# Adding the pixel to a depthwise convolution in PSUM by a second matmul, in a windowed-attention kernel

## The chip, the cores and the metric

The kernel runs on one core of a Trainium2 chip. The metric is device time in microseconds of one execution. All times below are medians of executions in the undisturbed ("fast") state unless said otherwise. Engines are named as the profile names them: PE is TensorE's matmul, PEld its weight load, DVE is VectorE, ACT is ScalarE, POOL is GpSimd, SP is SyncE. A matmul has a stationary operand (its weights, loaded first) and a moving operand (the columns streamed past them); its sums land in PSUM, and copying them out of there is called an evacuation. The granted clock is the share of TensorE's full clock that the profile shows.

## The reference

An image of 511 x 511 pixels with 192 channels goes through a 3 x 3 depthwise convolution that is added to it, a layer norm, attention with 4 heads inside windows of 7 x 7 pixels, an output projection, and a residual addition:

```
x0 = x + depthwise3x3(x, dw_pe)          # this case is about this line
h  = layernorm(x0)
qkv = windows(h) @ w_qkv                 # 73 x 73 windows of 49 tokens
out = softmax(q @ k.T * scale) @ v @ w_o
return x0 + unwindow(out)
```

All inputs are bf16.

## The kernel before

The 5329 windows are handled in 42 blocks of 128. While a block goes through attention in groups of 8 windows, the next block's convolution and statistics are slipped in between. Two copies of x are loaded for a block:

- `XP`, by plane: 81 partitions (the 9 x 9 pixels that a window's convolution touches), then 128 windows, then 192 channels. It feeds the convolution.
- `XC`, by token: 128 partitions (windows), then 49 tokens, then 192 channels. The convolution is added to it, giving x0.

The convolution of one channel is one matmul: the stationary operand is `XP[0:81, :, c]`, 128 weights that lie 192 elements (384 bytes) apart, and the moving operand is a tap matrix of 81 x 49. Twenty channels share a PSUM tile (there are four tiles for the whole kernel), and VectorE adds the tile to `XC`:

```python
def load_xc(blk):
    ...   # 16 windows at a time, on the GpSimd queue
    nc.gpsimd.dma_start(out=xc[...], in_=xw[a, b0 + o : b0 + o + nb])

def conv_tile(blk, it):
    ...
    ps = PS.next()
    for cc in range(ncn):
        nc.tensor.matmul(ps[:, col : col + S], lhsT=XP[0:KP, :, c], rhs=T[0:KP, c, :], start=True, stop=True)
    nc.vector.tensor_tensor(out=xc[...], in0=<the PSUM tile>, in1=xc[...], op=ALU.add)
    ...
```

`XC` has two buffers, so the load for a block waits until the store of the block two before it has left the buffer, and VectorE's addition waits for the load.

## Time and profile before

| | before |
|---|---|
| time, median of 2 | 5348.66 us (5340.74 to 5356.59) |
| busy share PE / DVE / ACT / POOL | 84% / 72% / 51% / 14% |
| mean granted clock | 0.824 |
| convolution matmuls, each with its own load | 8064 |
| DMA moved | 375 MB |

The busy shares are averages over stages with different limits. One block of some 127 us has a convolution stage in which TensorE is busy nearly all the time (38.22 of 39 us in the block read below), and an attention stage in which TensorE, VectorE and ScalarE take turns. The prediction below shows the lines and how they are read.

### The profile page before, as it was taken

The page shows a single profiled execution, that of the slowest core. Times are in us where ns is not written, and L with a number is a line of the kernel's source. Part 1 is how long each engine was busy: PE and PEld are TensorE (multiplying, and loading weights), DVE is VectorE, ACT ScalarE, POOL GpSimd, SP SyncE. Part 2 cuts the span into 40 slices and gives each one's busy share as a digit, 9 for nine tenths or more (in the row PEclk, how much of TensorE's full clock was granted, in tenths as well). Part 3 has the DMA queues.
Part 4 walks back from the last instruction along what each step waited for, and adds up shares of the span by engine and source line. Part 5 has one row for each costly group of instructions (what it writes and reads, how often), then busy time and mean ns, then how long its engine had stood idle before and what let it go on. Part 6 is the DMA issues. An engine that isn't in the chain of part 4 may idle for free.

```text
span 5337.2 us, 148265 instructions
## 1 busy us (share of the span) xinstructions
PE 4490.1 (84%) x65427; PEld 3661.5 (69%) x65427; DVE 3816.7 (72%) x6912; ACT 2744.5 (51%) x3385; POOL 758.0 (14%) x833
## 2 busy tenths in 40 slices
PE   2788888888888888888988888888888888888887
PEld 1666676667776676677776777767666776677776
DVE  6776777767776777777677777777777777767776
ACT  1554555545555555555555455555555555545555
POOL 1111111111111111111111111111111111111120
PEclk9887888887778887888788877788888888877888
DMA  6554445554455555554455544455555445544431
GB/s 67 51 75 70 68 71 80 82 73 68 68 68 70 71 72 74 71 74 71 68 73 91 75 68 68 68 72 72 74 72 72 73 70 78 85 74 67 68 48 32
DMA packets 512613, 375.27 MB, mean 70 GB/s; under 512 B 453129, under 2 KB 453321, under 8 KB 511958
## 3 DMA queue, kind: packets, MB, share of 16 engines
q1 hardware_dynamic: 480918, 265.08, 38.1%
q0 software_dynamic: 30592, 100.32, 10.6%
q8 instruction: 514, 8.42, 0.7%
q14 instruction: 141, 1.16, 0.1%
q10 hardware_dynamic: 448, 0.30, 0.0%
HBM read 265.31 MB, written 100.27 MB: 68 GB/s over the span
## 4 chain that ended last, share of the span: by engine, by line
PE 44%; DVE 16%; ACT 14%; DMA 12%; SPq 9%; issue 4%; POOL 1%; DVEq 0%; ACTq 0%; POOLq 0%
PE ps L412 12%; PE ps L282 8%; SPq L396 7%; DMA out_dram<-XC 7%; PE ps L369 6%; DMA XC<-in_x_dram 5%; PE ps L453 5%; PE ps L532 4%; DVE kT L424 4%; ACT hT L355 4%; DVE Qb L422 3%; PE ps L431 2%; DVE XC L284 2%; PE ps L560 2%; ACT kT L426 2%
## 5 line engine op out<-in xcount | busy, mean ns | idle before, releaser
L412 PE MATMUL ps<-hT,Wqk 96*128 96x392 bf16 x5336 | 1233.5, 380 | 76.7 <-DVE XC L284 62.2
L478 ACT ACTIVATE PT<-ps 128x784 bf16<-128x784 f32 x667 | 552.7, 829 | 1095.3 <-PE ps L453 1080.3
L421 ACT CAST Qb<-ps 64x784 bf16<-64x784 f32 x667 | 555.3, 833 | 657.5 <-PE ps L412 655.7
L412 PEld LDWEIGHTS <-Wqk 96*128 96x128 bf16 x5336 | 529.4, 108 | 486.1 <-issue 252.5
L284 DVE TENSOR_TENSOR XC<-ps,XC 128x980 bf16<-128x980 f32 x378 | 437.9, 1176 | 503.0 <-PE ps L282 247.2
L282 PE MATMUL ps<-T,XP 81*128 81x49 bf16 x8064 | 744.0, 264 | 55.5 <-DMA XP<-in_x_dram 55.5
L567 ACT CAST OT<-ps 96x784 bf16<-96x784 f32 x667 | 541.0, 811 | 456.0 <-PE ps L560 452.4
L282 PEld LDWEIGHTS <-XP 81*128 81x128 bf16 x8064 | 733.9, 220 | 57.6 <-issue 55.5
L431 PE MATMUL ps<-Wv,hT 96*128 96x192 bf16 x5336 | 663.5, 277 | 16.4 <-DVE On L544 9.0
L532 PE MATMUL ps<-V,PT 49*64 49x49 bf16 x21344 | 542.5, 195 | 159.1 <-DVE Qb L422 81.2
L431 PEld LDWEIGHTS <-hT 96*128 96x128 bf16 x5336 | 548.8, 111 | 180.0 <-issue 91.6
L544 DVE TENSOR_TENSOR On<-ps,rs 128x768 bf16<-128x768 f32 x667 | 634.6, 951 | 16.0
L532 PEld LDWEIGHTS <-PT 49*64 49x64 bf16 x21344 | 466.2, 116 | 260.4 <-issue 217.7
L327 POOL TENSOR_TENSOR D<-ident,rstd 128x896 bf16<-128x896 bf16 x294 | 486.2, 1681 | 1074.8 <-DVE rstd L320 1053.3
L424 DVE CAST kT<-ps 128x784 bf16<-128x784 f32 x462 | 450.0, 974 | 219.2 <-PE ps L412 209.1
L304 DVE BATCH_NORM_STATS2 bnst<-XC 128x6 f32<-128x192 bf16 x2058 | 600.5, 343 | 0.2
L453 PE MATMUL ps<-Qb,kT 128*64 128x98 bf16 x10672 | 408.0, 225 | 180.7 <-DVE Qb L422 132.2
L422 DVE CAST Qb<-ps 64x784 bf16<-64x784 f32 x462 | 451.6, 978 | 110.6 <-ACT Qb L421 100.1
L355 ACT CAST hT<-ps 96x896 bf16<-96x896 f32 x462 | 452.4, 1109 | 135.9 <-PE ps L346 134.9
L560 PE MATMUL ps<-ident,On 128*96 128x98 bf16 x5336 | 412.1, 226 | 114.4 <-DVE kT L424 110.9
L453 PEld LDWEIGHTS <-kT 128*64 128x64 bf16 x10672 | 341.5, 121 | 231.5 <-issue 131.7
L108 POOL DMA_DIRECT2D XC<-in_x_dram x386 | 216.0, 560 | 1865.9 <-DVE rs L543 996.3
(73 smaller groups left out, 4396.2 us busy)
## 6 DMA issues: line engine op xcount, KB each, us to landing
XC<-in_x_dram POOLq DMA_DIRECT2D x277, 294.0 KB, 7.5
out_dram<-XC SPq DMA_DIRECT2D x277, 294.0 KB
XP<-in_x_dram SPq DMA_DIRECT2D x210, 246.4 KB
XP<-in_x_dram SPq DMA_DIRECT2D x68, 243.0 KB
XC<-in_x_dram POOLq DMA_DIRECT2D x37, 165.4 KB, 7.1
out_dram<-XC SPq DMA_DIRECT2D x37, 165.4 KB
XP<-in_x_dram SPq DMA_DIRECT2D x22, 216.0 KB
XP<-in_x_dram SPq DMA_DIRECT2D x18, 212.6 KB
```

Of the source, the lines that this page charges most:

```text
L282: nc.tensor.matmul(ps[:, col : col + S], lhsT=XP[0:KP, :, c], rhs=T[0:KP, c, :], start=True, stop=True)
L304: nc.vector.bn_stats(out=bnst[:, s, :], in_=xc[:, s, :])
L355: nc.scalar.copy(out=hv[0:KT, kt, :, s0 : s0 + NDG], in_=src)
L412: nc.tensor.matmul(ps[:, ab * 512 : ab * 512 + TOK], lhsT=Wqk[kt][0:KT, which * 2 + ab, :], rhs=hT[0:KT, kt, ck * CH : (ck + 1) * CH, 0:S] ...
L421: nc.scalar.copy(out=dst[0:64, :, :, 0, :], in_=src[0:64])
L422: (nc.vector.tensor_copy if dve_help else nc.scalar.copy)(out=dst[64:128, :, :, 1, :], in_=src[64:128])
L424: nc.vector.tensor_copy(out=dst[:, :, 0:TOK], in_=two_bank(ps, TOK))
L431: nc.tensor.matmul(ps[:, col : col + C], lhsT=hT[0:KT, kt, ck * CH + 2 * jj : ck * CH + 2 * jj + 2, :].rearrange("p w s -> p (w s)"), rhs= ...
L453: nc.tensor.matmul(ps[64 * wp : 64 * wp + 64, col : col + 2 * S], lhsT=k_[:, ab, w * S : w * S + 64], rhs=q_[:, ab, w, :, :].rearrange("p ...
L478: nc.scalar.activation(out=pt[:, 0 : 16 * S].rearrange("p (b n) -> p b n", b=2), in_=two_bank(ps, 8 * S), func=ACTF.Exp, scale=scale,)
L532: nc.tensor.matmul(ps[64 * wp : 64 * wp + 64, col : col + S], lhsT=pt[64 * wp : 64 * wp + S, pc_ : pc_ + 64], rhs=v_[64 * wp : 64 * wp + S ...
L544: nc.vector.tensor_tensor(out=o_[:].rearrange("p (b j) (h d) -> p b (j h) d", b=2, d=DH), in0=ov[:, :, :, 0:DH], in1=r_[:].rearrange("p (b ...
```

## The change

Its intent: let TensorE add the pixel while the convolution is still in PSUM. Then x need not be loaded a second time by token, VectorE's addition becomes a plain copy, and half of the copies can go to ScalarE. The core of the diff:

```diff
-    load_xc(0)
     load_xp(0)
...
+    Cen = consts.tile([128, S], BF, name="Cen")      # 81 x 49: a 1 where the row is the token's own pixel
+    nc.gpsimd.memset(Cen[:], 1.0)
+    nc.gpsimd.affine_select(out=Cen[:], in_=Cen[:], compare_op=ALU.is_equal, fill=0.0, base=10, ...)
...
-                nc.tensor.matmul(ps[:, col : col + S], lhsT=XP[0:KP, :, c], rhs=T[0:KP, c, :], start=True, stop=True)
+                nc.tensor.matmul(ps[:, col : col + S], lhsT=XP[0:KP, :, c], rhs=T[0:KP, c, :], start=True, stop=False)
+                nc.tensor.matmul(ps[:, col : col + S], lhsT=XP[0:KP, :, c], rhs=Cen[0:KP, :], start=False, stop=True)
+            cp = nc.scalar.copy if it % 2 else nc.vector.tensor_copy
             if ncn == 20:
-                nc.vector.tensor_tensor(out=xc[...], in0=two_bank(ps, ...), in1=xc[...], op=ALU.add)
+                cp(out=xc[...], in_=two_bank(ps, ...))
...
-                if blk + 1 < NBLK:
-                    load_xc(blk + 1)
```

More of the change, by code (lines that the diff above doesn't have):

```diff
@@ L53, in _window_attn_kernel @@
     outr = out[0].rearrange("(a r) (b q) c -> a b r (q c)", r=WS, q=WS)
-    xw = x[0].rearrange("(a r) (b q) c -> a b r (q c)", r=WS, q=WS)
     consts = ctx.enter_context(tc.tile_pool(name="consts", bufs=1))
@@ L101, in segments @@
         return segs
-    def load_xc(blk):
-        xc = XC[blk % 2]
-        for (a, b0, b1, p0) in segments(blk):
-            for o in range(0, b1 - b0, 16):
-                nb = min(16, b1 - b0 - o)
-                nc.gpsimd.dma_start(
-                    out=xc[p0 + o : p0 + o + nb].rearrange("p (r q) c -> p r (q c)", q=WS), in_=xw[a, b0 + o : b0 + o + nb]
-                )
     def load_xp(blk):
@@ L183, in _window_attn_kernel @@
     nc.vector.memset(XC[1][:], 0.0)
+    Cen = consts.tile([128, S], BF, name="Cen")
+    nc.gpsimd.memset(Cen[:], 1.0)
+    nc.gpsimd.affine_select(out=Cen[:], in_=Cen[:], compare_op=ALU.is_equal, fill=0.0, base=10, pattern=[[1, WS], [9, WS]], channel_multiplier=-1)
     Wqk = [consts.tile([128, 4, 128], BF, name=f"Wqk{kt}") for kt in range(2)]
@@ L281, in conv_tile @@
                 col = (cc // 10) * 512 + (cc % 10) * S
-                nc.tensor.matmul(ps[:, col : col + S], lhsT=XP[0:KP, :, c], rhs=T[0:KP, c, :], start=True, stop=True)
+                nc.tensor.matmul(ps[:, col : col + S], lhsT=XP[0:KP, :, c], rhs=T[0:KP, c, :], start=True, stop=False)
+                nc.tensor.matmul(ps[:, col : col + S], lhsT=XP[0:KP, :, c], rhs=Cen[0:KP, :], start=False, stop=True)
+            cp = nc.scalar.copy if it % 2 else nc.vector.tensor_copy
             if ncn == 20:
-                nc.vector.tensor_tensor(
+                cp(
                     out=xc[:, :, c0 : c0 + 20].rearrange("p s (b c) -> p b s c", b=2),
-                    in0=two_bank(ps, 10 * S).rearrange("p b (c s) -> p b s c", s=S),
-                    in1=xc[:, :, c0 : c0 + 20].rearrange("p s (b c) -> p b s c", b=2),
-                    op=ALU.add,
+                    in_=two_bank(ps, 10 * S).rearrange("p b (c s) -> p b s c", s=S),
                 )
@@ L293, in conv_tile @@
                     cs = c0 + bk * 10
-                    nc.vector.tensor_tensor(
+                    cp(
                         out=xc[:, :, cs : cs + nn],
-                        in0=ps[:, bk * 512 : bk * 512 + nn * S].rearrange("p (c s) -> p s c", s=S),
-                        in1=xc[:, :, cs : cs + nn],
-                        op=ALU.add,
+                        in_=ps[:, bk * 512 : bk * 512 + nn * S].rearrange("p (c s) -> p s c", s=S),
                     )
@@ L605, in main @@
             if nb < NBLK:
-                if blk == 0 and ck == 0:
-                    load_xc(nb)
                 i0 = (ck - CONV0) * CPS
```

## The prediction

> **What bounds the kernel now.** I read the head of the page and the clock first, then the groups by line, then one block in the timeline, because an 84% TensorE says nothing about which stage is bound by it.
>
> ```profile
> PE 4490.1 (84%) x65427; PEld 3661.5 (69%) x65427; DVE 3816.7 (72%) x6912; ACT 2744.5 (51%) x3385; POOL 758.0 (14%) x833
> ```
>
> TensorE is the busiest engine. What matters more for this change is that the counts of PE and PEld are equal: every matmul carries its own weight load, so a second matmul on the same weights should bring a second load. The groups that the change touches:
>
> ```profile
> L284 DVE TENSOR_TENSOR XC<-ps,XC 128x980 bf16<-128x980 f32 x378 | 437.9, 1176 | 503.0 <-PE ps L282 247.2 <-DMA XC<-in_x_dram 215.9 <-issue 40.0
> L282 PE MATMUL ps<-T,XP 81*128 81x49 bf16 x8064 | 744.0, 264 | 55.5 <-DMA XP<-in_x_dram 55.5
> L282 PEld LDWEIGHTS <-XP 81*128 81x128 bf16 x8064 | 733.9, 220 | 57.6 <-issue 55.5
> ```
>
> The convolution is 8064 matmuls (42 blocks of 192 channels). VectorE does wait 215.9 us for the loads of x by token, and that is the wait the change is aimed at. The wait list says how much of it reaches TensorE:
>
> ```profile
> PE ps L412 <- DVE XC L284: 62.2, 36, 5.7
> ```
>
> Only 62.2 us in 36 waits. Next, TensorE's timeline in one block's convolution stage (start, length, what):
>
> ```profile
> 2065.24 7.31 PE L282 MATMUL ps<-T,XP 81*128 81x49 bf16 x80
> 2073.02 1.47 PE L412 MATMUL ps<-hT,Wqk 96*128 96x392 bf16 x4 [0.47 <-DVE XC L284]
> ...
> 2087.58 5.50 PE L282 MATMUL ps<-T,XP 81*128 81x49 bf16 x60
> 2092.91 2.79 PE L412 MATMUL ps<-hT,Wqk 96*128 96x392 bf16 x8
> ...
> 4571.02 5.53 PE L282 MATMUL ps<-T,XP 81*128 81x49 bf16 x60
> 4576.37 2.79 PE L412 MATMUL ps<-hT,Wqk 96*128 96x392 bf16 x8
> ```
>
> While the load was under way TensorE filled all four PSUM tiles with 80 convolution matmuls and lost 0.47 us. Then it runs without gaps. The stretch table (length, busy time of PE, PEld, DVE, ACT, POOL, granted clock, DMA share, GB/s) makes the stage plain:
>
> ```profile
> 2065.00:2104.00 39.00, 38.22 (x398) 31.38 (x395) 22.76 (x26) 7.21 (x9) 1.00 (x4) 0.50 0.16 26
> 2104.00:2128.00 24.00, 16.09 (x292) 12.11 (x289) 19.41 (x71) 17.78 (x23) 4.91 (x3) 0.93 0.75 62
> ```
>
> So the convolution stage is **TensorE's stage**: busy 38.22 of 39 us, at half the clock, with VectorE and ScalarE far below it. It takes 39 of the roughly 127 us of a block (5337 / 42). The change adds work to the one engine that is full there.
>
> **The price of one convolution matmul** is not the 264 ns of its row (these overlap), but the distance from start to start. Between 2087.58 and 2092.91, 60 of them took 5.33 us: 88.8 ns. The lines at 4571 show the same 60 in 5.35 us (89.2 ns), and there the clock was granted in full, where those at 2087 ran at half:
>
> ```profile
> 4571.00:4575.00 4.00, 3.98 (x45) 4.00 (x46) 1.00 0.02 4
> 2089.00:2092.00 3.00, 3.00 (x36) 3.00 (x36) 0.50 0.02 5
> ```
>
> (The table is of line 282 alone.) A price that doesn't move when the clock doubles isn't the streaming of 49 columns. It is the load of 128 weights, which XP gives with a step of 192 elements: 88.8 / 128 = 0.69 ns a column. I take it that loads follow one another at this pace and the short matmuls hide behind them.
>
> **What the Trainium skill says.** Page "TensorE: Matmul & The Clock Gate", section "LDWEIGHTS (loading the stationary operand)": a load costs about its number of columns over 1.2 GHz, 107 ns for 128, whatever the contraction is; the section after it, "Weight-path perf modes — Fast Weight Load (FWL) and DoubleRow", has about 2x measured for full 128-column bf16 weights. The 88.8 ns here lie between the two, so I use the trace. Either way a load of 128 columns outlasts 49 streamed columns. The same page, "Part 1: The HAM clock gate", gives two clock states, half and full, set by activity in windows of about 3.4 us. The trace agrees on the states (0.50 and 1.00), and shows that convolution work pulls the clock down: the stretch at 4571 began at 1.00, and the projection after it took 2.79 us for 8 matmuls against 1.53 us elsewhere at full clock. "VectorE: DVE Perf Modes", section "Mode 2×_2P — use both read ports for one tensor", says that PSUM has one read port for VectorE, so a copy out of PSUM can't use that mode. The trace agrees: casts of 784 elements take 974 ns, the addition of 980 takes 1176, a difference of 1.03 ns per element. A copy of 980 will not beat the addition it replaces. "ScalarE: Activation LUTs", section "What ACT_TABLE_LOAD costs", has 186 + 0.833 ns per element with immediates: an estimate of 1002 ns for 980. ScalarE's 784-element casts measured 811 to 833 ns here, in step with it.
>
> **The change part by part.**
>
> Added on TensorE: 8064 matmuls and, by the equal counts, 8064 loads of the same strided weights. At 88.5 ns (rounded over several stretches) that is 17.0 us for each block of 192, and 8064 x 88.5 ns = **+713.7 us**. Where does it lie? In blocks 1 to 41 in the stage that is 98% TensorE, and in block 0 in the opening, where 192 of them take 17.23 us with nothing beside them. So nearly all counts.
>
> Removed: the wait for x by token. Its full value to TensorE is the row above: **-62 us**. The other 150 us of VectorE's wait are hidden behind convolution matmuls already. Something of the wait must remain: the copies still write the buffer that the store of the block before reads. But the stores had all landed at about 2063 with the loads beside them and would land sooner alone, while the first copies come at about 2068.8 (20 pairs of 177 ns after 2065.24). No wait should be left.
>
> Removed in the opening: the load of block 0 by token shares the queues with the nine-plane load of XP. The first convolution waits until 109.8 us. There the issue of XP runs from 18.4 to about 101 us, against 50.5 us for 27 such issues in the middle of the kernel. Without the companion, XP could be in at about 77 us, and VectorE's clearing of buffers ends at 79.5. I take **-25 us**, a little less than the 30 that would follow.
>
> Moved: 10 evacuations a block are split. VectorE loses half of 438 us, which it did not need in this stage (22.76 of 39 us busy). ScalarE gains five or six copies of about 1 us a block, into a stage where it has 7.21 of 39 us of work. Nothing on the path.
>
> Sum: 5348.7 + 713.7 - 62 - 25 = **5975 us**, about 11.7% slower.
>
> **Rivals.**
>
> *The second load is free.* If the build kept one load for both matmuls, or the array skipped it, the added 41 ns (49 columns at half clock) would fit under the load of the next channel. The time would be 5348.7 - 62 - 25, about 5260 us, within 2%. For it: the operand is literally the same. Against it: the equal counts, in a kernel where nobody asked for sharing and where each matmul call left one load. I see no call in the diff that asks for it now. 4%.
>
> *The clock comes up.* More matmuls could keep the array active, and the stage's other TensorE work (39 - 17 = 22 us a block, all at half clock) would take half: -11 us a block, some -450 us, for a time near 5520, still slower. For it: the clock stands at 1.00 at the start of some convolution stretches. Against it: the share of streaming in the mix stays the same, 49 columns for each 88.5 ns, and the opening's convolution kept its 89 ns pace too. Longer stretches of such work should hold the clock down more surely, which may cost 20 to 50 us in the blocks where it came up between them.
>
> *The removed transfer was worth more.* The chain of waits shows 5.9% of its length, about 315 us, on the load of XC, another 8.3% on the issue of the stores. If this were all on the path, the sum would be near 5720. Against it: that chain follows VectorE, and TensorE ran convolution matmuls for 7.31 us at the same time. A chain's share is not what its removal gives when another engine fills the gap.
>
> **Range and chances.** The main term can miss by the pace: 85 to 91 ns gives 685 to 734 us. The wait and the opening are worth between 30 and 130 us together, and the clock may cost up to 50 or give some 50. Range 5880 to 6060. Slower by over 2% unless the load is free: 0.95; within 2%: 0.03; faster by over 2%: 0.02.
>
> **What would show it.** In the changed profile: 16128 convolution loads and as many matmuls, at 177 ns a channel, in stretches of about 10.6 us where there were 5.3; the stage 39 us becoming about 55 us with TensorE still at 98% and the clock at 0.50; no wait of line 412 on the evacuation; VectorE's copy still near 1.18 us and ScalarE's near 1.0; the first convolution starting near 80 us. The prediction is wrong if PEld's count stays near 65427, if a channel takes well under 150 ns for its two matmuls, or if the clock in the stage rises to 1.00.

## The result, and the profile after

The changed kernel takes **5947.25 us** (2 runs, 5935.76 to 5958.74) against 5348.66. The ratio is 1.1111, with a 95% interval of 1.1039 to 1.1183. Ratios here and below are taken over fast runs of the same rounds, so they differ slightly from the ratio of the medians quoted. The prediction was 5975 us, in a range of 5880 to 6060.

First the page of the changed kernel: the engine line, then the groups of the convolution (line, engine, operation, count, busy time, mean of one in ns, idle time just before them):

```profile
PE 5255.5 (88%) x73491; PEld 4429.1 (74%) x73491; DVE 3630.8 (61%) x6660; ACT 2943.3 (49%) x3637; POOL 542.1 (9%) x449
...
L276 PEld LDWEIGHTS <-XP 81*128 81x128 bf16 x8064 | 1442.5, 217 | 20.6 <-issue 15.0
L277 PE MATMUL ps<-Cen,XP 81*128 81x49 bf16 x8064 | 1455.8, 263 | 0.0
L277 PEld LDWEIGHTS <-XP 81*128 81x128 bf16 x8064 | 1446.6, 218 | 0.0
...
L280 DVE CAST XC<-ps 128x980 bf16<-128x980 f32 x210 | 247.3, 1178 | 1030.8 <-PE ps L277 1030.8
...
L280 ACT CAST XC<-ps 128x980 bf16<-128x980 f32 x168 | 163.9, 976 | 1077.4 <-PE ps L277 1077.4
```

PE and PEld both rose by 8064: the second matmul brought a second load of the same 128 weights. VectorE's copy takes 1178 ns, as long as the addition it replaced, and ScalarE's 976 ns. Both engines now wait for TensorE, 1030.8 and 1077.4 us.

Second, TensorE's timeline. The end of the convolution stage of the block that the prediction read in the kernel before:

```profile
2099.38 1.22 PE L282 MATMUL ps<-T,XP 81*128 81x49 bf16 x12
2100.41 2.79 PE L412 MATMUL ps<-hT,Wqk 96*128 96x392 bf16 x8
```

The same stage of one block of the changed kernel, its first convolution matmul and its end:

```profile
2275.91 0.29 PE L276 MATMUL ps<-T,XP 81*128 81x49 bf16 x1
...
2327.07 0.26 PE L277 MATMUL ps<-Cen,XP 81*128 81x49 bf16 x1
2327.16 2.79 PE L404 MATMUL ps<-hT,Wqk 96*128 96x392 bf16 x8
```

From the first convolution matmul to the projection that follows the last one it was 35.17 us (2065.24 to 2100.41). Now it is 51.25 us, 16.1 us more. The block is no exception: from the first to the last start of a convolution matmul, the stages of blocks 1 to 41 add up to 1466 us in the trace before and 2096 us after, and the time between the stages hardly changed (3543 and 3550 us). The table of stretches shows who is busy there (length, then busy time of PE, PEld, DVE, ACT, POOL, then granted clock, DMA share, GB/s):

```profile
2275.00:2327.00 52.00, 51.37 (x595) 46.78 (x595) 17.48 (x20) 10.38 (x12) 0.00 (x0) 0.54 0.01 1
```

TensorE is busy for 51.37 of 52 us at a clock of 0.54, VectorE for 17.48, ScalarE for 10.38. It is still TensorE's stage, only longer.

Third, the opening, where block 0's convolution has no other work beside it. Before, then after:

```profile
109.83 17.23 PE L282 MATMUL ps<-T,XP 81*128 81x49 bf16 x192 [55.51 <-DMA XP<-in_x_dram]
```

```profile
69.33 0.20 PE L276 MATMUL ps<-T,XP 81*128 81x49 bf16 x1 [15.02 <-DMA XP<-in_x_dram]
```

Without the companion load, XP is there 40.5 us earlier. The 384 matmuls that follow take 34.4 us where 192 took 17.23:

```profile
69.30:104.00 34.70, 34.39 (x384) 34.38 (x385) 13.72 (x15) 4.61 (x6) 0.21 (x1) 1.00 0.01 1
```

The clock of 1.00 in this line, and in the tables of the opening below, is no measurement: the trace's first record of the clock begins at 128.8 us (in the other runs at 108 us or later), and the table shows 1.00 where there is none.

### The profile page after: what moved, and what is told of

Same layout as the page of the kernel before. It is cut to its first block, busy times and chain, and to the rows that moved or that the text cites. A ratio compares the mean times of both kernels' runs of the same rounds, so it can differ in the third digit from the quotient of the medians.

```text
span 5957.0 us, 162994 instructions
## 1 busy us (share of the span) xinstructions
PE 5255.5 (88%) x73491; PEld 4429.1 (74%) x73491; DVE 3630.8 (61%) x6660; ACT 2943.3 (49%) x3637; POOL 542.1 (9%) x449
## 4 chain that ended last, share of the span: by engine, by line
PE 65%; DVE 18%; ACT 14%; issue 2%; SPq 1%; POOL 0%; DMA 0%; DVEq 0%; ACTq 0%; POOLq 0%
PE ps L404 17%; PE ps L276 12%; PE ps L277 12%; DVE Qb L414 7%; DVE kT L416 7%; PE ps L524 6%; PE ps L361 6%; PE ps L445 6%; ACT hT L347 5%; ACT Qb L413 2%; ACT kT L418 2%; PE ps L423 2%; ACT Qb L414 2%; PE ps L369 2%; PE ps L552 1%
## 5 line engine op out<-in xcount | busy, mean ns | idle before, releaser
L276 PE MATMUL ps<-T,XP 81*128 81x49 bf16 x8064 | 1458.8, 265 | 15.1 <-DMA XP<-in_x_dram 15.0
L276 PEld LDWEIGHTS <-XP 81*128 81x128 bf16 x8064 | 1442.5, 217 | 20.6 <-issue 15.0
L277 PE MATMUL ps<-Cen,XP 81*128 81x49 bf16 x8064 | 1455.8, 263 | 0.0
L277 PEld LDWEIGHTS <-XP 81*128 81x128 bf16 x8064 | 1446.6, 218 | 0.0
L404 PE MATMUL ps<-hT,Wqk 96*128 96x392 bf16 x5336 | 1270.4, 388 | 10.6 <-ACT hT L347 6.9
L280 DVE CAST XC<-ps 128x980 bf16<-128x980 f32 x210 | 247.3, 1178 | 1030.8 <-PE ps L277 1030.8
L423 PE MATMUL ps<-Wv,hT 96*128 96x192 bf16 x5336 | 688.9, 282 | 8.6 <-DVE On L536 4.7
L280 ACT CAST XC<-ps 128x980 bf16<-128x980 f32 x168 | 163.9, 976 | 1077.4 <-PE ps L277 1077.4
L423 PEld LDWEIGHTS <-hT 96*128 96x128 bf16 x5336 | 564.4, 113 | 173.2 <-issue 87.0
L445 PEld LDWEIGHTS <-kT 128*64 128x64 bf16 x10672 | 353.9, 122 | 224.8 <-issue 136.4
```

Source lines behind the costliest of these rows:

```text
L404: nc.tensor.matmul(ps[:, ab * 512 : ab * 512 + TOK], lhsT=Wqk[kt][0:KT, which * 2 + ab, :], rhs=hT[0:KT, kt, ck * CH : (ck + 1) * CH, 0:S] ...
L423: nc.tensor.matmul(ps[:, col : col + C], lhsT=hT[0:KT, kt, ck * CH + 2 * jj : ck * CH + 2 * jj + 2, :].rearrange("p w s -> p (w s)"), rhs= ...
L445: nc.tensor.matmul(ps[64 * wp : 64 * wp + 64, col : col + 2 * S], lhsT=k_[:, ab, w * S : w * S + 64], rhs=q_[:, ab, w, :, :].rearrange("p ...
```

## The experiments

The main theory: **the weight load is the price**. A load of 128 weights spaced 384 bytes apart takes 88.5 ns, loads follow one another at that pace, and 49 streamed columns hide behind them. The rivals: the streaming or the second accumulation costs; or the removed transfers were worth more, and the second matmul cost more, than I counted. Twelve kernels were run, each timed in three rounds against the kernel before on the same chip, so each ratio is to that kernel.

One direct test could not be made: two matmuls on one load. The language used here gives each matmul its own load. The runs with wider streams stand in for it. Where the expectations reckon a streamed column, the traces give the same: at half clock eight matmuls of 392 columns took 2.59 us (2100.41 to 2103.00 in the kernel before), 0.83 ns a column, so an estimate of some 40 ns for 49 columns.

### Without the second matmul

```diff
-                nc.tensor.matmul(..., rhs=T[0:KP, c, :], start=True, stop=False)
-                nc.tensor.matmul(..., rhs=Cen[0:KP, :], start=False, stop=True)
+                nc.tensor.matmul(..., rhs=T[0:KP, c, :], start=True, stop=True)
```

> The changed kernel without the second matmul: the pixel is never added, so the result is wrong on purpose; loads by token and VectorE addition stay away. It measures all that the removals gave. My theory (each added load cost 88.5 ns, and the removed wait reached TensorE for some 62 us plus the opening): 5947 - 714 = about 5235 us, ratio near 0.978 to the kernel before, and a convolution stage of 38 to 39 us a block again. Rival (the removed transfers were worth the 5.9% that the chain showed, or more, and the second matmul cost correspondingly more): near 5030 us. Second rival (the removals gave nothing): 5349 us.

Measured: 5233.55 us, ratio 0.9785 (0.9735 to 0.9835); the result is wrong. The opening's convolution is back at its old length:

```profile
72.82 17.25 PE L276 MATMUL ps<-T,XP 81*128 81x49 bf16 x192 [18.51 <-DMA XP<-in_x_dram]
```

So the change is the sum of two: the removals give 0.0215 of 5343 us, some 115 us, and the second matmul takes 1.1111 - 0.9785 = 0.1326, some 709 us; by the intervals these may be off by some 27 and 47 us. The estimate of 8064 x 88.5 ns was 713.7. In the traces the 41 stages add up to 1392 us without the second matmul and 2096 with it: 704 us, 17.2 a stage. The rival that the removed transfers were worth the 315 us of the chain falls.

### The second matmul streams 8 columns

```diff
-                nc.tensor.matmul(ps[:, col : col + S], ..., rhs=Cen[0:KP, :], start=False, stop=True)
+                nc.tensor.matmul(ps[:, col : col + 8], ..., rhs=Cen[0:KP, 0:8], start=False, stop=True)
```

> The changed kernel with the second matmul streaming 8 columns in place of 49, its weight load kept (wrong result on purpose). If the load is the price, nothing moves: about 5947 us, within 1%, and still 177 ns a channel. If streaming or the accumulation into the same PSUM columns is the price, some 5/6 of the added 714 us goes: near 5350 us.

Measured: 5908.51 us, ratio 1.1076 (1.1018 to 1.1135), which overlaps the changed kernel's 1.1111 (wrong result). Five sixths of the added streaming are gone and nothing moved. In the opening (PE busy and PEld busy of the first matmuls' line, clock, DMA):

```profile
66.00:102.00 36.00, 34.11 (x192) 34.07 (x192) 1.00 0.01 2
```

The 192 channels still take 34.11 us, 178 ns each. Streaming is not the price.

### The second load from weights that lie together

```diff
-                nc.tensor.matmul(..., lhsT=XP[0:KP, :, c], rhs=Cen[0:KP, :], start=False, stop=True)
+                nc.tensor.matmul(..., lhsT=ident[0:KP, :], rhs=Cen[0:KP, :], start=False, stop=True)
```

> The changed kernel, but the second matmul loads its 128 weights from the identity tile, where they lie next to one another, in place of XP with its step of 192 elements (wrong result on purpose). If 128 columns are the price whatever their layout, nothing moves: about 5930 us and 177 ns a pair. If the step is a large part of the price, the added load becomes short and the streaming of 49 columns (41 ns at half clock) is what remains: a pair near 130 ns, 8064 x 41 = about 330 us over the run without the second matmul, near 5565 us.

Measured: 5459.22 us, ratio 1.0207 (1.0184 to 1.0231), wrong. Still 8064 added loads of 128 columns, but they cost 1.0207 - 0.9785 = 0.0422, some 225 us or 28 ns each, less than a third of the strided ones and less than I expected. The same line of the opening:

```profile
68.00:93.00 25.00, 23.20 (x192) 23.20 (x192) 1.00 0.02 4
```

A pair takes 121 ns, where two strided loads take 178. So the number of weight columns loaded does not make the price, and neither does anything else that an added matmul of 49 columns brings, its issue or its adding to the same sums: all of it together is within these 28 ns (32 in the opening). The identity tile is also the same tile every time, so this run alone doesn't tell weights that lie together from weights that were read just before; but in the changed kernel too each second load reads the very weights of the load before it, and there it cost 89 ns. The runs with a padded step, below, bear out the step.

### The pixel folded into the tap weights

```diff
         nc.sync.dma_start(out=dwK[9 * j : 9 * j + 3, :], in_=dw_pe[:, j, :])
+    one10 = consts.tile([32, 1], F32, name="one10")       # 1 in row 10, the centre tap, else 0
+    ...
+    nc.vector.tensor_scalar(out=dwK[:], in0=dwK[:], scalar1=one10[:, 0:1], scalar2=None, op0=ALU.add)
...                                                        # and one matmul a channel, no Cen
```

> One matmul a channel again: 1 is added to the centre tap in the small weight tile before the tap matrices are built, so the pixel comes with the convolution; loads by token and VectorE addition stay away, ScalarE copies half. Load theory: as without the second matmul, about 5235 us, 2% faster than before. The rounding of 1 + w to bf16 may or may not pass the comparison; I expect it to pass with a somewhat larger error. Rival as for the run without the second matmul: 5349 or 5030 us.

Measured: 5211.28 us, ratio 0.9754 (0.9709 to 0.9799), correct. All that the change aimed at is there, and TensorE pays nothing for it. The centre weight is now 1 + w rounded to bf16, which drops low bits of w.

### One load, twice the columns

```diff
-                nc.tensor.matmul(ps[:, col : col + S], lhsT=XP[0:KP, :, c], rhs=T[0:KP, c, :], start=True, stop=True)
+                n2 = 2 * S if cc % 10 < 9 and cc + 1 < ncn else S
+                nc.tensor.matmul(ps[:, col : col + n2], lhsT=XP[0:KP, :, c], rhs=<taps of c and c + 1>, start=True, stop=True)
```

> The folded kernel, but each convolution matmul streams 98 columns (its own channel's 49 and the next channel's 49, which the next matmul overwrites), with one weight load as before: the array work of the changed kernel without its second load. Load theory: 98 columns at half clock take 82 ns, under the 88.5 ns of a load, so the time stays within 1% of the folded kernel. Streaming theory: 9 of 10 channels pay 41 ns more, 8064 x 0.9 x 41 = near 300 us more, about 5530 us. If more streaming keeps the clock up in the stage, it could be faster than the folded kernel, down to some 4900 us.

Measured: 5141.45 us, ratio 0.9618 (0.9566 to 0.967), correct. It carries the array work of the changed kernel on one load a channel, and it is not only not slower than the folded kernel but 1.4% faster, with intervals apart. In the opening, the first 132 channels, up to TensorE's first wait, run at the pace of the folded kernel. The folded kernel first, then this one:

```profile
64.32 11.96 PE L276 MATMUL ps<-T,XP 81*128 81x49 bf16 x132 [9.94 <-DMA XP<-in_x_dram]
```

```profile
65.77 11.93 PE L277 MATMUL ps<-T,XP 81*128 81x98 bf16 x132 [11.40 <-DMA XP<-in_x_dram]
```

Twice the columns behind one load: 11.93 against 11.96 us. With the narrow run this closes the question of load or stream. The gain comes with a higher mean clock, 0.861 against 0.834 in the profiled runs, which led to the next two.

### Three and four channels' columns per load

The edit is the same with 147 and 196 columns.

> The folded kernel with three channels' columns (147) streamed per load, of which the next matmuls overwrite two thirds (correct result). The run with 98 columns was faster than the folded kernel (0.9618 against 0.9754) with a higher mean clock (0.861 against 0.834); this tells whether the streaming does that. If streaming keeps the clock up in the convolution stage: 147 columns take 61 ns at full clock, still under the 88.5 ns load, and the rest of the stage runs at full speed, so clearly faster than 5141 us, down to about 4900, mean clock over 0.90. If the clock stays at half in the stage, 122 ns exceed the load, and 8064 x 0.8 x 34 = about 220 us are added: near 5430 us.

> As the run before with four channels' columns (196) per load. If the clock is up through the whole stage: 82 ns, still under a load, the same time as with three, near 4900 us. If it is up only in part: slower than with three, since at half clock 196 columns take 163 ns, at worst 5211 + 8064 x 0.7 x 75 = about 5630 us.

Measured: 147 columns 5120.53 us, ratio 0.9578 (0.9552 to 0.9604), mean clock 0.908; 196 columns 5315.13 us, ratio 0.9919 (0.9856 to 0.9981), mean clock 0.877; both correct. In one block with 147 columns, TensorE's timeline (lines left out between):

```profile
2072.06 9.09 PE L277 MATMUL ps<-T,XP 81*128 81x147 bf16 x80
...
2093.72 5.57 PE L277 MATMUL ps<-T,XP 81*128 81x147 bf16 x60
2099.14 1.52 PE L404 MATMUL ps<-hT,Wqk 96*128 96x392 bf16 x8
```

The clock in the two stretches shown (the table is of line 277 alone):

```profile
2072.00:2081.00 9.00, 8.94 (x80) 8.96 (x80) 0.53 0.01 2
2094.00:2099.00 5.00, 5.00 (x59) 5.00 (x58) 1.00 0.01 3
```

The stage's first stretch runs at some 111 ns a matmul (8.9 us for 80, up to the next matmul at 2080.97), near the 122 ns of 147 columns at half clock (some of the 80 stream fewer columns). Later ones run at 90 to 95 ns, near a load's pace, and the projection takes 1.52 us where it took 2.79 in the same place before. So streaming more per load does bring the clock up inside the stage: its mean over the 41 stages is 0.54 with 49 columns, 0.58 with 98, 0.73 with 147 and 0.65 with 196. The changed kernel, with 49 columns for each of its loads, shows 0.55. The gain itself lies after the stages. Against the folded kernel's trace, the stages changed by -10 us with 98 columns, +7 with 147 and +202 with 196, the time between them by -44, -94 and -79. My 4900 us was too hopeful: the first stretch pays at half clock, and with 196 columns this payment is more than the gain.

### The second matmul without the removals

```diff
-                nc.tensor.matmul(..., rhs=T[0:KP, c, :], start=True, stop=True)
+                nc.tensor.matmul(..., rhs=T[0:KP, c, :], start=True, stop=False)
+                nc.tensor.matmul(..., lhsT=XP[0:KP, :, c], rhs=Zer[0:KP, :], start=False, stop=True)   # zeros; loads and addition stay
```

> The kernel before with its loads by token and its VectorE addition kept, and a second matmul with a zero matrix added to each channel (correct result): the addition of the change without its removals. Load theory: +714 us; the wait for the loads, 62 us on TensorE, should vanish by itself, since a PSUM tile now takes 3.5 us to fill and four of them cover the wait; the opening's 40 us are still paid. So 5343 + 714 - 62 = about 5995 us, some 50 us above the changed kernel. Rival (the removals are worth over 100 us beside a slow convolution too): 6057 us or more.

Measured: 6029.8 us, ratio 1.1291 (1.1266 to 1.1317), correct. Its wait list has 1.3 us of TensorE's waiting on the addition, where the kernel before had 62.2; the wait for x by token vanished behind the longer filling of PSUM, without its load being removed. Left is the opening (second line):

```profile
PE ps L415 <- DVE XC L287: 1.3, 1, 1.3
PE ps L284 <- DMA XP<-in_x_dram: 54.9, 1, 54.9
```

That is 54.9 us against 15.0 in the changed kernel, 40 us of the difference. The whole difference to the changed kernel is 1.1291 - 1.1111 = 0.018, some 96 us by the ratios, 59 us between the two profiled runs. The changed kernel was timed only twice, so whether 20 or 55 us beyond the opening are real stays open. In the traces they don't lie in the convolution stages, which add up to 2100 us here and 2096 there; the time between the stages is 3570 and 3550 us.

### The parts of the removal alone

Folded, with all copies on VectorE:

```diff
-            cp = nc.scalar.copy if it % 2 else nc.vector.tensor_copy
+            cp = nc.vector.tensor_copy
```

> The folded kernel with all evacuations of the convolution on VectorE, none on ScalarE. If the stage is TensorE's, the split is worth nothing: 5211 us within 0.5%. Rival (VectorE's turn comes late and holds PSUM tiles): 20 to 60 us slower than the folded kernel.

Measured: 5201.15 us, ratio 0.9734 (0.9718 to 0.975), inside the folded kernel's interval. ScalarE's half is worth nothing that these runs can tell.

The kernel before without its loads by token (all calls of `load_xc` taken out; VectorE adds what is there, so the result is wrong):

> The kernel before without its loads by token; the VectorE addition stays and adds what lies in the buffer (wrong result on purpose). If the removed gain is the wait for the loads and the opening alone, it equals the run without the second matmul: 5343 - 62 - 40 = about 5240 us. If the ScalarE half or the copy in place of the addition gave part of it, it stays above: near 5300 us.

Measured: 5214.96 us, ratio 0.9756 (0.9739 to 0.9772). Taking the loads away gives the whole gain of the removals by itself, within the intervals; the copy in place of the addition, and the share for ScalarE, add nothing that shows.

### The step between the weights

The folded kernel, with XP's rows padded; only the declaration and the loads' destination change:

```diff
-    XP = big.tile([128, BLK, C], BF, name="XP")
+    XP = big.tile([128, BLK, C + 8], BF, name="XP")        # C + 16 in the second run
```

> The folded kernel with each window's row of XP padded from 192 to 200 elements, so that the weights lie 400 bytes apart in place of 384 (correct result). If the 88.5 ns come from the particular step, the load gets shorter and conv matmuls approach the 28 to 45 ns that an added contiguous load cost: some 200 to 300 us faster than the folded kernel. If any step away from contiguous costs the same, the time stays at 5211 us within 1%.

> The folded kernel with XP's rows padded to 208 elements: a step of 416 bytes, where 384 bytes gave 88.5 ns a channel and 400 bytes gave 62 ns. If it is 384 that is bad (a multiple of 128 and of 64 bytes, which neither 400 nor 416 is), 416 does as well as 400: about 4990 us, 62 ns. If the largest power of two in the step counts by degrees (384 = 3 x 128, 416 = 13 x 32, 400 = 25 x 16), it lies between: 5050 to 5150 us. If 400 is good for another reason and 416 is as bad as 384: 5211 us.

Measured: a step of 400 bytes 4993.95 us, ratio 0.9354 (0.932 to 0.9389); a step of 416 bytes 5177.94 us, ratio 0.9695 (0.9674 to 0.9717), one of whose six runs was slow and is in neither figure (the median of all six is 5185.76). Both correct. The opening of the first, then of the second:

```profile
71.67 8.28 PE L276 MATMUL ps<-T,XP 81*128 81x49 bf16 x132 [16.76 <-DMA XP<-in_x_dram]
```

```profile
67.94 10.74 PE L276 MATMUL ps<-T,XP 81*128 81x49 bf16 x132 [12.51 <-DMA XP<-in_x_dram]
```

Against 11.96 us with a step of 384. Less the length of the last matmul (about 0.25 us), over 131 starts: 89 ns at 384 bytes, 80 ns at 416, 61 ns at 400. For 400 bytes, the 28 ns saved, times 8064, are 226 us, and the folded kernel minus this one is 5211 - 4994 = 217 us; in the traces the 41 stages are 219 us shorter and the time between them is the same. For 416 bytes, 9 ns times 8064 are 73 us, but only 33 us came (5211 - 5178), less than either theory that gives it a gain. The profiled run, the fastest of its six at 5134.55 us, has the 73 us in full: it is 74 us under the folded kernel's profiled run, and its stages are 85 us shorter. Its mean clock was 0.836; the other fast runs had 0.812 to 0.823, where the folded kernel's had 0.829 to 0.834. So in that run the load's gain was there; in the others what was missing came with a lower clock, whose cause stays open. That the shorter pace is due to the load's reading of memory is argued from the step being the only thing changed. Why 400 is best of the three (25 x 16, where 416 is 13 x 32 and 384 is 3 x 128, so the order fits the largest power of two in the step) would need more steps to show. The padded, folded kernel beats both kernels: 6.5% under the kernel before.

## Why the prediction was right, point by point

- **The second load is not shared.** Right: 73491 loads for 73491 matmuls, and the narrow and the wide stream show that the load alone is paid.
- **+713.7 us on the path.** Right: some 709 us by the run without the second matmul, 17.2 us more in the opening, and 17.2 us more a stage against that run (17.0 predicted).
- **The pace doesn't depend on the clock.** Right in the block read at full clock, and over the whole trace before: starts of neighbouring convolution matmuls lie 89.4 ns apart on average at a recorded clock of 1.00 (539 of them) and 88.7 ns at 0.50 (7167). The run with 147 columns agrees: 90 ns a matmul behind which the projection ran at full clock. The pace in the opening, which the prediction also names, shows nothing of the clock, as that has no record there.
- **The removed wait, -62 us, and the opening, -25 us.** The mechanism was right and the sizes too small. The opening gave 40.5 us: XP was in before VectorE's clearing ended, and the first matmuls need no VectorE, so the clearing that I set as a limit was none. All removals together gave 115 us by the run without the second matmul, so 74 us for the wait and what else follows (its 41 stages are 74 us shorter than before, 1466 to 1392). That is 28 us more than the 87 predicted, within the 30 to 130 that the range allowed, and as much as the whole miss, 5975 to 5947. The run with the zero matmul adds a point that the prediction missed: the wait was going to vanish in any case, since a slower convolution covers it. That part of the saving belongs to neither half of the change alone.
- **The split of the copies costs and gives nothing.** Right; 5201 against 5211 us.
- **The rival of the removed transfer.** It falls, with a misreading: the 5.9% and the 8.3% are shares of the chain between 2000 and 2360 us. Over the whole execution the load of XC has 4.9%, about 262 us, and the issue of the stores 7.2%. The removals gave 115 us, well under either.
- **The rival of the clock.** It did not happen in the changed kernel (0.54 in the stage, predicted 0.50). The reason given, that the share of streaming stays the same, is not shown to be the cause: with 8 columns in the second matmul the share fell, and the clock over the stages stayed at 0.55. The runs with wider streams show that the mechanism exists.
- **What I took as given and did not question** was the 88.5 ns. I read it as the price of 128 strided weights, and it was the price of this one step; a padding of 16 bytes takes it to 61.

## What to carry to other kernels

Price a short matmul by the distance from start to start, and ask what sets it. Here it moved neither with the clock nor with the columns streamed, but with the layout of the weights: it was the weight load, and a second matmul on the same weights cost as much as the first. Before moving an addition to the engine that is already full in its stage, look whether it can be folded into an operand that is loaded anyway, here into the centre tap. Where the stationary operand is read with a step, try padding the step by some bytes: here it was worth more than the whole change was after.

## What the Trainium skill lacked or had wrong

- "TensorE: Matmul & The Clock Gate", section "LDWEIGHTS (loading the stationary operand)", gives the cost by the number of columns alone, and section "Weight-path perf modes — Fast Weight Load (FWL) and DoubleRow" admits packed or strided weights alike. Here the same 128 bf16 weights took 89 ns a load at a step of 384 bytes, 80 at 416 and 61 at 400, and an added load of weights that lie together (the same tile each time) cost 28 ns. The dependence on the step is in neither.
- The same page, "Part 1: The HAM clock gate", explains the clock by how busy TensorE is in windows of some 3.4 us. Here TensorE was busy for 51.37 of 52 us at a clock of 0.54. What raised the mean clock was more columns per load: 0.834 with 49, 0.861 with 98, 0.908 with 147 (and 0.877 with 196, at a longer time). So TensorE's busy share in a profile does not tell its clock; which activity counts, no run here settles.
- No page says that a trace may have no record of the clock in its opening. Here the first record begins at 108 us or later in every trace looked at, and the profile shows 1.00 before it; yet in the opening of the run with 147 columns most of the matmuls start 121 to 125 ns apart, the pace of half clock, where stretches at a recorded 1.00 showed 90.
